# Nyström attention, layer norm and MLP on one core: group 1's transposes moved from DMA to TensorE, k sums of three batches moved from VectorE to GpSimd, and part of the schedule reordered

## The chip, the core and the metric

The kernel runs on one core of a Trainium2 chip. A core has five engines with a queue of instructions each: TensorE (PE in the profile, with its weight loads shown apart as PEld), VectorE (DVE), ScalarE (ACT), GpSimd (POOL) and SyncE (SP), which here issues all DMA transfers. An engine works through its own queue in order and waits where an operand or a buffer is not there yet. The metric is the device time of the core in microseconds (us) for one execution, as a median of repeated runs; 347.5 us before (347.33 to 348.74 in three runs).

## What is computed

Inputs are q, k, v of shape (8, 8, 576, 64) (batches, heads, rows, head size), a scale g of 512, and weights of 512x2048 and 2048x512, all fp32. The reference, cut to what matters:

```python
q_lm = q.reshape(B, H, 32, 18, D).mean(axis=3)       # 32 landmarks, each the mean of 18 rows
k_lm = k.reshape(B, H, 32, 18, D).mean(axis=3)
A  = softmax(q @ k_lm.T / 8)                          # 576 x 32
Bm = softmax(q_lm @ k_lm.T / 8)                       # 32 x 32
C  = softmax(q_lm @ k.T / 8)                          # 32 x 576
Z  = Bm.T / (norm_1(Bm) * norm_inf(Bm))
for _ in range(6):
    Z = 2 * Z - Z @ Bm @ Z
attn = A @ Z @ C @ v                                  # heads are then laid side by side: x is (8, 576, 512)
xn = (x - mean(x)) / sqrt(var(x) + 1e-6) * g_ln       # over the 512 columns
out = x + relu(xn @ w_ch1) @ w_ch2                    # 512 -> 2048 -> 512
```

## The kernel before, in words

The 8 x 576 = 4608 rows of x are cut into 36 blocks of 128 rows (`xblk`), and four blocks make a group: 9 groups for the MLP. A batch of 576 rows is 4.5 blocks. A unit (U = 2 per batch) is half a batch's heads, four heads.

**The MLP stream.** `mlp()` is a generator that runs group after group. For a group it needs the four centred blocks (`xn`) turned so that the 512 columns lie on partitions (`xnT`). Then come 16 x 4 matmuls into `psh` (w_ch1; ACT writes relu of it as `hT`) and 4 x 16 matmuls into `pso` (w_ch2; DVE adds x into `ot`, SP stores it). Each `next` of the generator places about one matmul on PE; `fill(n)` takes n of them. The program thus lays MLP matmuls between the steps of the attention, and the tables `counts` say how many stand after each step. Since every engine keeps program order (`keep_in_program_order`), this writing order is the order of the queues.

**Turning the rows.** Group 0's four blocks are turned by PE (`transpose_block`: four 128x128 transposes into the PSUM tile `psxt`, and a DVE copy into `xnT`). The blocks of all other groups are turned by a DMA transpose (`turn_by_dma`), issued on SP in program order among the loads of q, k and v and the stores of the result. `psh` of a group is not placed before all four turns of it are placed, and reads all four.

**The attention.** Batches 0 and 1 go through `attention`: PE turns q and k (`pst`, with their landmark sums in `pss`), ACT copies them out as `xT`. Batches 2 | 3, 4 | 5, 6 | 7 are four sets that go through `attention2`. For a set, `Coming` prepares the inputs: SP loads a part (one unit of k, q or v) into one of 6 `stg` buffers, POOL casts it to fp16 (`nat`, 8 buffers, or `natv`), DVE turns it (`turn`: `xT`), and the landmark sums are made: those of q by five POOL additions (`asum`, `s16`), of which DVE turns the small result; those of k by one DVE reduction (`add_up`: `lmk`). `next_cast` places one cast (and one load ahead of it), `next_job` one `turn` or `add_up`; the loop over `sets` calls both after each step of the set before. In `attention2` come first the scores (`psb`, `psec`, exponentials on ACT, `bm` and `ecT` on DVE), then `psse` and `pscv`, then six steps of the iteration (`psn` on PE, `st` and `ebd` on DVE, each needing the one before; `psea` and its exponential in the first), `pszc`/`zcbd`, and the rows of the batch (`psy` on PE, `xblk` on DVE).

**Layer norm.** When a block of rows is whole, `block_done` places its mean and variance and its centring. Blocks 4 to 7 (group 1) are done by ACT in `center_by_act`: a mean pass and a subtraction (`xn`), and a pass of squares (`junk`) for the variance. Later blocks with an even number are summed by ACT in two passes (`stats_by_act`), the others by DVE (`bn_stats`), and POOL centres them (`center`). `deviations` (ACT: `lnv`, `rstd`) gives a group's scales, needed by its `ot`. What is placed on the list `later` is written out by `settle()` after the step.

**The start.** Ahead of the sets stands an order written out by hand: the steps of batch 0 (`a0`), batch 1 (`a1`), `scale_w1` (w_ch1 times g, cast to fp16 in slices of 256 columns by ACT and POOL) and `fill`. For group 0 a `psh` tile holds 2 x 256 columns and takes 8 matmuls.

## Time and profile before

| | |
|---|---|
| time, median of 3 runs | 347.5 us (347.33 to 348.74) |
| the profiled execution's own time | 347.76 us |
| its span (first to last instruction) | 345.9 us |
| PE busy | 317.6 us, 92% of the span |
| DVE, ACT, POOL busy | 183.0, 148.9, 136.1 us |
| mean granted TensorE clock | 0.979 of full speed |

The span lies 1.9 us under the execution's own time. The page cuts the span into 40 slices of 8.6 us and gives each engine's busy share in tenths; the windows view gives busy time, count of instructions and granted clock (PEclk) for stretches that one chooses. The timeline lists instructions in order of time as: start, duration, engine, line, operation, output and inputs, count, and in brackets how long the engine sat idle before it and what ended that. Nearly all instructions are recorded through helpers, so they bear the lines 67 (other engines) or 73 (PE), and have to be told apart by their tiles' names. Rows of one kind in a run are merged; the duration of a merged row of matmuls has the tail of the pipeline in it.

### The profile page before, as it was taken

To read this page: it belongs to the slowest core of one execution; us is meant where nothing else is said; L and a number is where in the kernel's file an instruction comes from. 1 tells how busy PE (TensorE), PEld (TensorE's weight loads), DVE (VectorE), ACT (ScalarE), POOL (GpSimd) and SP (SyncE) were. 2 spreads that over 40 slices of the span, in tenths; PEclk is the share of its full clock that TensorE was granted. 3 is DMA by queue.
4 is the path that set the end of the run, shared out by engine and by line. 5 is a ranking of instruction groups with operands and counts; after the bars stand their busy time and mean duration, and the time that the engine had idled before them with its cause. 6 is when DMAs were issued, how large, how long until landed. Compare 5 with 4: busy or idle time off the path is not lost.

```text
span 345.9 us, 8196 instructions
## 1 busy us (share of the span) xinstructions
PE 317.6 (92%) x3396; PEld 158.9 (46%) x3396; DVE 183.0 (53%) x393; ACT 148.9 (43%) x294; POOL 136.1 (39%) x214
## 2 busy tenths in 40 slices
PE   7787989686899999699999999999999999999994
PEld 6545764232344544244454544545444444444441
DVE  2556569562996738998454656872346510020011
ACT  3339855901546057027830474465116405504600
POOL 3488879999999829623101001430002300000000
PEclk9989999986999999999999999999999999999999
DMA  7999999999798886027102401450135034022023
GB/s 269 366 355 364 348 408 288 291 284 310 266 353 120 241 213 181 0 59 139 31 4 63 96 2 27 95 79 17 30 73 81 0 81 88 15 61 63 0 53 68
DMA packets 38932, 50.86 MB, mean 147 GB/s; under 512 B 20464, under 2 KB 24560, under 8 KB 38896
## 3 DMA queue, kind: packets, MB, share of 16 engines
q1 hardware_dynamic: 38896, 50.35, 51.6%
q8 instruction: 26, 0.43, 0.5%
q14 instruction: 10, 0.08, 0.1%
HBM read 36.70 MB, written 9.44 MB: 133 GB/s over the span
## 4 chain that ended last, share of the span: by engine, by line
PE 66%; DVE 14%; ACT 4%; DMA 2%; POOL 2%; issue 2%; SPq 0%; POOLq 0%
PE psh L73 31%; PE pso L73 28%; DVE ebd L67 3%; DVE st L67 2%; DVE xT L67 2%; PE pscv L73 2%; DMA stg<-in_v_dram 2%; PE psy L73 2%; DVE lmk L67 2%; DVE xblk L67 1%; ACT xn L67 1%; POOL asum L67 1%; PE psec L73 1%; PE psea L73 1%; POOL nat L67 1%
## 5 line engine op out<-in xcount | busy, mean ns | idle before, releaser
L73 PE MATMUL psh<-xnT,w 128*128 128x512 f16 (+1 forms) x640 | 136.4, 361 | 5.8 <-issue 4.3
L67 ACT ACTIVATE hT<-psh 128x512 f16<-128x512 f32 x144 | 85.1, 597 | 121.1 <-PE psh L73 120.6
L73 PE MATMUL pso<-w,hT 128*128 128x512 f16 x576 | 133.0, 381 | 0.0
L73 PEld LDWEIGHTS <-w 128*128 128x128 f16 x640 | 59.8, 98 | 62.3 <-issue 9.3
L73 PEld LDWEIGHTS <-hT 128*128 128x128 f16 x576 | 54.9, 98 | 61.3 <-issue 2.6
L67 DVE SCALAR_TENSOR_TENSOR ot<-pso,rstd,xblk 128x512 f32<-128x512 f32 x36 | 26.9, 748 | 80.4 <-PE pso L73 80.3
L67 POOL CAST nat<-stg 128x1152 f16<-128x1152 f32 x28 | 32.3, 1169 | 3.9 <-DMA stg<-in_k_dram 1.9
L67 POOL CAST natv<-stg 128x1152 f16<-128x1152 f32 x16 | 18.4, 1172 | 31.9 <-PE pscv L73 21.7
L67 DVE TENSOR_TENSOR xblk<-psy,rcpd 128x512 f32<-128x512 f32 (+1 forms) x40 | 27.6, 691 | 2.1
L67 DVE SCALAR_TENSOR_TENSOR st<-st,psn 128x192 f16<-128x192 f16 (+3 forms) x36 | 14.3, 397 | 23.0 <-PE psn L73 23.0
L67 POOL TENSOR_SCALAR negm<-mvg 128x1 f32<-128x1 f32 x18 | 3.5, 192 | 55.1 <-DVE mvg L67 46.6
L67 DVE TENSOR_TENSOR ebd<-st,mask 128x256 f16<-128x256 f16 (+1 forms) x30 | 22.7, 756 | 1.0
L67 POOL TENSOR_TENSOR asum<-asum 128x256 f32<-128x256 f32 (+2 forms) x36 | 20.4, 566 | 2.8
L67 POOL TENSOR_SCALAR xn<-xblk,mvg 128x512 f16<-128x512 f32 x10 | 6.9, 694 | 35.8 <-ACT junk L67 35.8
L73 PE MATMUL psy<-zcbd,ea 128*128 128x260 f16 (+1 forms) x80 | 16.5, 283 | 3.0 <-ACT xT L67 1.2
L67 DVE STREAM_TRANSPOSE xT<-nat 128x576 uint32<-128x576 uint32 x24 | 18.4, 766 | 0.0
L67 DVE TENSOR_REDUCE lmk<-xT 128x64 f16<-128x1152 f16 x12 | 16.1, 1342 | 0.1
L67 ACT ACTIVATE junk<-xblk 128x512 f16<-128x512 f32 x10 | 6.3, 628 | 22.4 <-DVE xblk L67 22.4
L67 POOL TENSOR_TENSOR asum<-nat 128x576 f32<-128x576 f16 x12 | 15.4, 1282 | 1.0
L67 DVE BATCH_NORM_STATS2 st<-xblk 128x6 f32<-128x512 f32 x22 | 15.2, 691 | 0.6
L67 POOL TENSOR_SCALAR xn<-xblk,negm 128x512 f16<-128x512 f32 x18 | 12.5, 694 | 3.3 <-DMA xnT<-xn 1.7
L73 PEld LDWEIGHTS <-ea 128*128 128x128 f16 (+1 forms) x80 | 7.2, 101 | 14.0 <-issue 4.9
(107 smaller groups left out, 247.7 us busy)
## 6 DMA issues: line engine op xcount, KB each, us to landing
stg<-in_q_dram SPq DMA_DIRECT2D x16, 576.0 KB, 6.8
stg<-in_k_dram SPq DMA_DIRECT2D x16, 576.0 KB, 7.8
out_dram<-ot SPq DMA_DIRECT2D x72, 128.0 KB, 2.4
stg<-in_v_dram SPq DMA_DIRECT2D x10, 576.0 KB, 7.5
w1stg<-in_moe_w_ch_dram SPq DMA_DIRECT2D x16, 256.0 KB, 6.1
w2stg<-in_moe_w_ch_dram SPq DMA_DIRECT2D x16, 256.0 KB, 4.9
stg<-in_v_dram SPq DMA_DIRECT2D x12, 288.0 KB, 6.5
xnT<-xn SPq DMA_TRANSPOSE x32, 3.4
```

The lines of the kernel that those rows point to most:

```text
L67: return lambda *args, **kw: keep(getattr(self.engine, op)(*args, **kw))
L73: keep(nc.tensor.matmul(o, l, r, start=start, stop=stop, tile_position=(rb, cb), skip_group_check=(skip or cb != 0)))
```

## The change

1. `center_by_act` no longer issues a DMA transpose for group 1. Its blocks are turned by PE in `transpose_block(1, u)`, from two places in `mlp()`: within the last two `pso` rows of group 0 at every eighth matmul, if the block's `xn` is placed, and ahead of group 1's `psh` otherwise. ACT copies these four `psxt` tiles into `xnT`. Each such turn takes one place in `fill`.
2. The squares of blocks 4 to 7, group 1's `deviations`, and the sums and the centring of block 8 are put on a list `late`, of which one entry is placed per step from step 3 of batch 2's `attention2` on.
3. For the sets (5, 6) and (7) the landmark sums of k are made by POOL as those of q are (`k_by_pool`). Their casts are spread over the steps of the set before (`spread`), none is placed earlier than that set, and their `turn` jobs begin at step 5 (before: step 1). `s16` has 8 buffers (before: 6). Before, `next_cast` went on to the set after the next when the next was done.
4. At the start, group 0's first three `psh` tiles and `scale_w1(0)` to `(2)` are placed ahead of most of batch 1's `pst`/`pss` steps, and the two rows of batch 0 that begin group 0 come first.
5. Four numbers of the second row of `counts` go from 17, 17, 17, 15 to 16, 16, 15, 14. `zeros` is half as wide, read more often to the same width.

The diff, without the lines for `zeros` and `s16`:

```diff
 
 
     class Coming:
-        def __init__(self, bs, first_by_pool=0):
-            self.bs, self.first_by_pool = bs, first_by_pool
+        def __init__(self, bs, k_by_pool=False):
+            self.bs, self.k_by_pool = bs, k_by_pool
             self.units = [(b, u) for b in bs for u in range(U)]
             pairs = [(w, w + 1) for w in range(0, len(self.units), 2)]
             self.parts = [(nm, w) for pair in pairs for nm in ("k", "q") for w in pair]
...
             for i, (nm, w) in enumerate(self.parts):
                 if nm != "v":
                     self.jobs.append((self.turn, i))
-                if nm == "k" or nm == "q" and w < first_by_pool:
+                if nm == "k" and not k_by_pool:
                     self.jobs.append((self.add_up, i))
+            self.done, self.turned = 0, set()
             self.stg, self.n16, self.sums, self.xT, self.lm = {}, {}, {}, {}, {}
 
+
+        def spread(self, step):
+            return self.done * 18 >= (step + 1) * len(self.parts)
+
         def next_job(self):
-            if self.jobs:
+            if self.jobs and (self.jobs[0][1] in self.n16 or self.jobs[0][1] in self.turned):
                 f, i = self.jobs.pop(0)
+                self.turned.add(i)
                 f(i)
 
         def load(self, i, queue=nc.sync):
...
                 self.lm = {nm: asm.tile([P, 4, LM, 2], FP16, name="lm" + nm,
                                         tag="lm" + nm) for nm in ("q", "k")}
             stg = self.stg.pop(i)
+            self.done += 1
             if nm == "v":
                 natv_of[b] = natv_buf[b % NV][:].rearrange("p a j e -> p (a j) e")
                 assert b - NV in v_used
...
             t = nat.tile([P, SEG, D], FP16, name="nat", tag="nat")
             pool.tensor_copy(out=t[:], in_=stg[:])
             self.n16[i] = t
-            if nm == "q" and w >= self.first_by_pool:
+            if nm == "q" or self.k_by_pool:
                 s = asum.tile([P, NJ, D], FP32, name="asum", tag="asum")
-                s16 = asm.tile([P, D], FP16, name="s16", tag="s16", bufs=6)
+                s16 = asm.tile([P, D], FP16, name="s16", tag="s16", bufs=8)
                 self.sums[i] = s16
                 for o, x, y in ((s[:], t[:, 0:9, :], t[:, 9:18, :]),
                                 (s[:, 0:4, :], s[:, 0:4, :], s[:, 4:8, :]),
...
             later.append(lambda: center_by_act(j))
         else:
             if by_act(j):
-                later.append(lambda: stats_by_act(j))
+                (late if j == 8 else later).append(lambda: stats_by_act(j))
             else:
                 stats(j)
-            later.append(lambda: center(j) if g <= mlp_at[0] + 1
+            (late if j == 8 else later).append(lambda: center(j) if g <= mlp_at[0] + 1
                          else uncentered.setdefault(g, []).append(j))
-        if u == 3:
+        if u == 3 and g != 1:
             later.append(lambda: deviations(g))
 
 
     mlp_at, uncentered = [0], {}
 
 
-    later = []
+    later, late = [], []
 
     def settle():
         while later:
...
         act(xn[:], x_blk[j][:], AF.Copy, scale=-1.0 / DM, accum_out=negm[:])
         act(xn[:], x_blk[j][:], AF.Identity, bias=negm[:], scale=1.0)
         if by_act(j):
-            junk = mxn.tile([P, DM], FP16, name="junk", tag="junk", bufs=1)
-            act(junk[:], x_blk[j][:], AF.Square, bias=negm[:],
-                accum_out=mvgs[g][:, u, 1:2])
-        if g > 0:
-            turn_by_dma(j)
+            def squares():
+                junk = mxn.tile([P, DM], FP16, name="junk", tag="junk", bufs=1)
+                act(junk[:], x_blk[j][:], AF.Square, bias=negm[:],
+                    accum_out=mvgs[g][:, u, 1:2])
+            late.append(squares)
+            if u == 3:
+                late.append(lambda: deviations(g))
 
     def center(j):
         g, u = divmod(j, 4)
...
     xnTs = {}
 
 
-    def transpose_block(u):
+    def transpose_block(g, u):
         if u == 0:
-            xnTs[0] = mxnT.tile([P, KCH, 512], FP16, name="xnT", tag="xnT")
-        xn = xn_of.pop(u)
+            xnTs[g] = mxnT.tile([P, KCH, 512], FP16, name="xnT", tag="xnT")
+        xn = xn_of.pop(4 * g + u)
         psxt = psM.tile([P, KCH, P], FP16, name="psxt", tag="pm")
         for c in range(KCH):
             TR(psxt[:, c, :], xn[:, ts(c, P)], ident16[:])
-        dve.tensor_copy(out=xnTs[0][:, :, ts(u, P)], in_=psxt[:])
+        if g == 0:
+            dve.tensor_copy(out=xnTs[g][:, :, ts(u, P)], in_=psxt[:])
+        else:
+            scalar.copy(xnTs[g][:, :, ts(u, P)], psxt[:])
+        turned.setdefault(g, []).append(u)
 
     turned = {}
 
...
                 for u in (0, 2):
                     if u == 0:
                         for i in range(2):
-                            transpose_block(i)
+                            transpose_block(0, i)
                             yield True
                     for m0 in range(0, MCH, 2):
                         if u == 0 and m0 in (6, 10):
-                            transpose_block(2 if m0 == 6 else 3)
+                            transpose_block(0, 2 if m0 == 6 else 3)
                             yield True
                         if u == 0 and m0 < MCH - 6:
                             scale_w1(m0 // 2 + 3)
...
                         yield True
             else:
                 while len(turned.get(g, ())) < 4:
-                    yield False
+                    u = len(turned.get(g, ()))
+                    if g == 1 and 4 + u in xn_of:
+                        transpose_block(1, u)
+                        yield True
+                    else:
+                        yield False
                 xnT = xnTs.pop(g)
                 for j in uncentered.pop(g + 1, ()):
                     center(j)
...
                        start=(m == 0), stop=(m == MCH - 1))
                     if m < MCH - 1:
                         yield True
+                    if g == 0 and u >= 2 and m % 8 == 3:
+                        n = len(turned.get(1, ()))
+                        if 4 + n in xn_of:
+                            transpose_block(1, n)
+                            yield True
                 ot = mout.tile([P, DM], FP32, name="ot", tag="ot")
                 dve.scalar_tensor_tensor(out=ot[:], in0=pso[:], scalar=rstds[g][:, u:u + 1],
                                          in1=x_blk.pop(j)[:], op0=ALU.mult, op1=ALU.add)
...
     for _ in range(6):
         run(a0)
         warm(1, 512)
-    run(a0, a1, a0, a0)
-    run(a1)
+    run(a0, a0, a0, a1)
     scale_w1(0)
     fill(1)
-    run(a0)
+    scale_w1(1)
+    fill(1)
+    scale_w1(2)
+    fill(4)
     run(a1)
-    fill(1)
-    scale_w1(1)
-    run(a1)
-    scale_w1(2)
+    fill(4)
+    run(a0, a1)
     fill(4)
     run(a0)
     fill(4)
     for _ in a0:
         pass
     run(a1)
-    fill(10)
+    fill(4)
+    run(a1)
+    fill(4)
     cast_v(1)
     fetch_w2()
     run(a1)
...
     settle()
 
 
-    sets = [Coming((2,)), Coming((3, 4)), Coming((5, 6)), Coming((7,))]
+    sets = [Coming((2,)), Coming((3, 4)), Coming((5, 6), True), Coming((7,), True)]
     to_load = [(c, i) for c in sets for i in range(len(c.parts))]
     to_cast = list(to_load)
 
...
 
 
     counts = [[10, 14, 14] + 6 * [6] + [4] + 3 * [6] + 2 * [9],
-              [12, 12, 17, 17, 17, 15] + 6 * [6] + [5] + 4 * [6] + 6 * [9],
+              [12, 12, 16, 16, 15, 14] + 6 * [6] + [5] + 4 * [6] + 6 * [9],
               [12, 12, 20, 20, 20, 17] + 6 * [9] + [9] + 10 * [8],
               [14, 21, 21] + 6 * [10] + [10] + 5 * [9]]
     for c, after, count in zip(sets, sets[1:] + [None], counts):
         for step, _ in enumerate(attention2(c.bs, c)):
             fill(count[step])
             settle()
-            next_cast()
-            if after and step >= 1:
+            if late and step >= 3:
+                late.pop(0)()
+            if after and after.done < len(after.parts) and not (
+                    after.k_by_pool and after.spread(step)):
+                next_cast()
+            if after and step >= (5 if after.k_by_pool else 1):
                 after.next_job()
         while after and after.jobs:
             fill(8)
```

How the queues move is shown at three places. The first is ACT at the start, from batch 0's first rows to the first `hT` and its follower (`xn` centres a block of group 0, `xT` is a turned q or k of batch 1 copied out, `w_16` a slice of w_ch1, `hT` the relu of a `psh` tile). Before:

```order
L67 COPY xT_746<-pst_736 128x1152
L67 ACTIVATE w1_16_157<-w1stg_162,g_sb_80 128x256
L67 ACTIVATE xn_777,negm_776<-xblk_769 128x512
L67 ACTIVATE xn_777<-xblk_769,negm_776 128x512
L67 COPY xT_790<-pst_780 128x1152
L67 ACTIVATE w1_16_157<-w1stg_166,g_sb_80 128x256
L67 COPY xT_830<-pst_811 128x1152
L67 ACTIVATE w1_16_157<-w1stg_170,g_sb_80 128x256
L67 ACTIVATE w1_16_157<-w1stg_174,g_sb_80 128x256
L67 ACTIVATE hT_761<-psh_840 128x2x256
```

Now:

```order
L67 ACTIVATE xn_699,negm_698<-xblk_690 128x512
L67 ACTIVATE xn_699<-xblk_690,negm_698 128x512
L67 COPY xT_725<-pst_715 128x1152
L67 ACTIVATE w1_16_157<-w1stg_162,g_sb_80 128x256
L67 ACTIVATE w1_16_157<-w1stg_166,g_sb_80 128x256
L67 ACTIVATE w1_16_157<-w1stg_170,g_sb_80 128x256
L67 ACTIVATE w1_16_157<-w1stg_174,g_sb_80 128x256
L67 ACTIVATE hT_740<-psh_766 128x2x256
L67 COPY xT_786<-pst_776 128x1152
```

The slices of w_ch1 and the first `hT` stand ahead of the copies of batch 1; on PE the first three `psh` tiles stand between batch 1's turns in the same way, and 44 instead of 34 of `psh`'s 256-column matmuls stand ahead of batch 1's `psb`, 76 instead of 64 ahead of its `psse`.

The second is ACT between block 7's centring and the first exponentials of batch 2. Before (`lnv` and `rstd` are group 1's deviations, the last two `junk` rows block 8's sums):

```order
L67 ACTIVATE xn,negm<-xblk 128x512
L67 ACTIVATE xn<-xblk,negm 128x512
L67 ACTIVATE junk,mvg<-xblk,negm 128x512
L67 ACTIVATE lnv<-mvg,eps_ln 128x2 x2
L67 ACTIVATE rstd<-lnv 128x4
L67 ACTIVATE junk,mvg<-xblk 128x512
L67 ACTIVATE junk,mvg<-xblk,mvg 128x512
L67 ACTIVATE psb<-psb 128x64
L67 ACTIVATE ec<-psec 128x576 x2
```

Now:

```order
L67 ACTIVATE xn,negm<-xblk 128x512
L67 ACTIVATE xn<-xblk,negm 128x512
L67 COPY xnT<-psxt 128x4x128
L67 ACTIVATE psb<-psb 128x64
L67 ACTIVATE ec<-psec 128x576 x2
L67 COPY xnT<-psxt 128x4x128 x3
L67 ACTIVATE hT<-psh 128x512 x2
L67 ACTIVATE ea<-psea 128x576 x2
L67 ACTIVATE hT<-psh 128x512
L67 ACTIVATE junk,mvg<-xblk,negm 128x512
```

The squares of blocks 4 to 6, each behind its own `xn` before, are gone from this stretch too; they come one at a time after batch 2's first `psea`. On PE the four turns of group 1 stand among the last 28 `pso` of group 0, the last of them four `pso` ahead of group 1's first `psh`; 9 `psh` (before: 7) stand ahead of batch 2's first `psn`. The four DMA_TRANSPOSE of group 1 are gone from SP.

The third is POOL, from the casts of batch 3's and 4's v on (`natv`). Before (`nat` begins the parts of batches 5 and 6; `xn` is block 8):

```order
L67 CAST natv1_115<-stg_1470 128x18x64
L67 TENSOR_SCALAR xn_1864<-xblk_1539,mvg_1546 128x512
L67 CAST natv1_115<-stg_1503 128x18x64
L67 CAST natv0_113<-stg_1535 128x18x64
L67 CAST natv0_113<-stg_1560 128x18x64
L67 CAST nat_1982<-stg_1650 128x1152
L67 CAST nat_2004<-stg_1771 128x1152
L67 CAST nat_2028<-stg_1878 128x1152
L67 TENSOR_TENSOR asum_2030<-nat_2028 128x576
```

Now (the `xn` are blocks 8 to 11):

```order
L67 CAST natv1_115<-stg_1469 128x18x64
L67 CAST natv1_115<-stg_1499 128x18x64
L67 CAST natv0_113<-stg_1528 128x18x64
L67 CAST natv0_113<-stg_1551 128x18x64
L67 TENSOR_SCALAR xn_2065<-xblk_1532,mvg_1539 128x512
L67 TENSOR_SCALAR negm_2089<-mvg_1539 128x1
L67 TENSOR_SCALAR xn_2091<-xblk_2071,negm_2089 128x512
L67 TENSOR_SCALAR xn_2115<-xblk_2095,mvg_1539 128x512
L67 TENSOR_SCALAR negm_2139<-mvg_1539 128x1
L67 TENSOR_SCALAR xn_2141<-xblk_2121,negm_2139 128x512
L67 CAST nat_2273<-stg_1646 128x1152
L67 TENSOR_TENSOR asum_2275<-nat_2273 128x576
```

The parts of batches 5 and 6 stand behind the centring of group 2, and each of their eight k and q parts is followed by its five additions. On DVE, four reductions of k are replaced by four turns of a 128x32 tile, and the last two turns of q stay where they were, behind the sixth `st` of batches 3 and 4.

6 lines of the change are left out of this document (3 added, 3 removed).

## The prediction

> **What bounds the kernel now.** I read the page's slices first: PE's busy tenths, and under them the granted clock.
>
> ```profile
> PE   7787989686899999699999999999999999999994
> PEclk9989999986999999999999999999999999999999
> ```
>
> PE is full from slice 12 (95 us) to the end, but for one 6 near 140 us; the last slice is the drain. Before that it has holes, and the clock falls to 8 and 6 in slices 9 and 10. The windows view says what the full part means:
>
> ```profile
> 180.00:190.00 10.00, 10.00 (x185) 4.97 (x184) 4.88 (x6) 0.00 (x0) 2.24 (x2) 1.00 0.24 54
> ```
>
> The columns are: stretch, its length, then PE, PEld, DVE, ACT, POOL busy (instructions), clock, DMA share, GB/s. PE is busy for all ten microseconds and nobody else is. So the end is set by PE's work plus PE's idle and slow time, and a change gains what it takes from the holes before 100 us and near 140 us, less what it adds to PE. The holes stand in PE's timeline:
>
> ```profile
> 64.21 2.33 PE L73 MATMUL pso<-w,hT 128*128 128x512 f16 x10
> 68.34 0.20 PE L73 MATMUL psse<-bm,bones 128*128 128x64 f16 x1 [1.80 <-DVE bm L67]
> ...
> 70.05 4.20 PE L73 MATMUL pso<-w,hT 128*128 128x512 f16 x14
> 74.18 0.89 PE L73 MATMUL pscv<-natv,ecT 32*32 32x65 f16 x72
> 75.00 1.68 PE L73 MATMUL pso<-w,hT 128*128 128x512 f16 x7
> 80.98 3.14 PE L73 MATMUL psh<-xnT,w 128*128 128x512 f16 x7 [4.30 <-issue]
> ...
> 84.22 1.16 PE L73 MATMUL psea<-xT,lmk 32*32 32x512 f16 x32
> ```
>
> There are two waits, 1.80 and 4.30 us, and behind each the same matmuls take longer. The windows of 1 us show why (clock is the third number from the end):
>
> ```profile
> 69.00:70.00 1.00, 0.88 (x72) 0.72 (x72) 0.90 (x5) 0.00 (x0) 0.84 (x3) 0.50 1.52 196
> 72.00:73.00 1.00, 1.00 (x5) 0.39 (x4) 0.65 (x1) 0.00 (x0) 0.92 (x2) 0.94 0.92 355
> 79.00:80.00 1.00, 0.00 (x0) 0.00 (x0) 0.00 (x0) 0.00 (x0) 0.92 (x2) 0.50 0.97 350
> 85.00:86.00 1.00, 1.00 (x27) 0.46 (x12) 0.82 (x2) 0.56 (x2) 0.84 (x3) 0.61 1.05 390
> ```
>
> The clock is halved from about 69 to 72 us and from 79 to 85.6 us, each time after a wait.
>
> What ends the waits? For the long one, SP's queue and the landing time of `xnT`:
>
> ```profile
> 64.83 1.75 SPq L822 DMA_TRANSPOSE xnT<-xn  x1
> ...
> 73.88 1.23 SPq L822 DMA_TRANSPOSE xnT<-xn  x1
> DMA to landing us min/median/max: 2.4/3.4/7.0
> ```
>
> Group 1's last transpose is issued at 73.88, among loads that wait for buffers, and lands up to 7.0 us later: 80.9, where `psh` starts. The profile calls this wait "issue"; the sum of issue and landing names it. For the short one, ACT's queue:
>
> ```profile
> 64.58 0.71 ACT L67 ACTIVATE junk<-xblk,negm 128x512 f16<-128x512 f32 x1
> ...
> 65.29 0.47 ACT L67 ACTIVATE lnv<-mvg,eps_ln 128x2 f32<-128x2 f32 x2
> ...
> 65.90 0.61 ACT L67 ACTIVATE junk<-xblk 128x512 f16<-128x512 f32 x1
> ...
> 67.36 0.20 ACT L67 ACTIVATE psb<-psb 128x64 f32<-128x64 f32 x1
> ```
>
> Batch 2's `psb` is on PSUM before the `pso` of 64.21, but its exponential waits behind squares, deviations and block 8's sums; `bm` and `psse` follow it.
>
> **The change part by part.** Three rows give full-clock prices: a 512-column matmul is 13.81/64 = 0.216 us (a row of the chain of waits), 32 score matmuls 0.70, a turn of one block 0.39 with its tail.
>
> ```profile
> 272.18 13.81 PE pso L73 x64
> 134.24 0.70 PE L73 MATMUL psea<-xT,lmk 32*32 32x512 f16 x32
> 27.99 0.39 PE L77 MATMUL psxt<-ident,xn 128*128 128x128 f16 x4
> ```
>
> *The short wait.* From 64.58 to 67.36 ACT now does 2.8 us that moves behind; one copy of a turned block comes in (0.6, as an `hT` of the same size). So `psb` comes 2.2 us earlier or more, over 1.80: the wait goes. With the wait goes the halved clock: 4.20 - 14 x 0.216 = 1.2 and 1.14 (the `pscv` at 68.97) is 0.25 over the 0.89 of its twin at 74.18. Gain 1.8 + 1.45. The moved passes land behind batch 2's `psea`, where ACT has waited for PE; the deviations are wanted only by group 1's `ot`, near 100 us.
>
> [...]
>
> *The long wait.* The transposes leave SP; PE turns the blocks. The last turn stands four `pso` (0.86 us) ahead of `psh`, and ACT's copy (0.6) fits in. Gain 4.3, and the halved clock behind it: 3.14 - 7 x 0.216 = 1.6, and 1.16 - 0.70 = 0.46. Together 6.4. What could be late next is the `xn` of block 7, which even now is done when its squares start at 64.58.
>
> *PE's new work.* Sixteen transposes: 4 x 0.24 (their weight loads alone) to 4 x 0.39. I take 1.2, nearer the lower end, since the tail overlaps what follows.
>
> *The start.* Here the trace shows the pieces but not their new order.
>
> ```profile
> 31.18 1.11 ACT L67 COPY xT<-pst 128x1152 f16<-128x1152 f16 x1
> 32.18 0.91 ACT L67 ACTIVATE w<-w1stg,g_sb 128x256 f16<-128x256 f32 x2
> ...
> 37.88 0.22 ACT L67 ACTIVATE psb<-psb 128x64 f32<-128x64 f32 x1
> 41.29 0.22 PE L73 MATMUL psse<-bmT 32*32 32x32 f16 x8
> 44.52 1.20 PE psh L73 x10
> ```
>
> (The first three rows are ACT's timeline, then PE's, then the chain of waits.) ACT is the bound here: before its `psb` it idles little. In the new order ACT begins with a block's `xn` at about 24.1 and has until `psb` three pairs of `xn` (1.45 each), four `xT` (1.0), eight `w` (0.45), five `hT` (0.5): 14.5 us, and I count 0.8 us of waiting for the first `psh` and for the third row of batch 0. So `psb` comes at 39.4, 1.5 later than now. Then 32 `psh` (now 30 and a turn, in 5.1 us) bring `psse` to 44.4, 3.1 later. Of these, 12 `psh` more are done, 12 x 0.12 = 1.45, which need not be done later. Lost: 1.65. The iteration of batch 1 then runs 3 us deeper into POOL's casts (one `ebd` of it takes 1.33 us beside them, others 0.43): 0.5. PE is sparser at 21 to 24, so the slower clock that slice 3 shows (8) may last longer: 0.3. I take a loss of 2.4. Bounds: a gain of 1.0, if the new order closes holes that PE has there now (the 8 and 7 of slices 3 and 4); a loss of 4.0, if the `xT` copies hold up the shared PSUM buffers once more.
>
> *k sums on POOL.* Two lines group what DVE loses and gets:
>
> ```profile
> L67 DVE TENSOR_REDUCE lmk<-xT 128x64 f16<-128x1152 f16 x12 | 16.1, 1342 | 0.1
> L67 DVE STREAM_TRANSPOSE lmq<-s 128x32 uint32<-128x32 uint32 x12 | 2.0, 168 | 0.0
> 142.02 0.34 PE L73 MATMUL psn<-st,ebd 128*128 128x96 f16 x4 [1.92 <-DVE ebd L67]
> ```
>
> Six of twelve reductions go, six small turns come. Only those inside the iteration of batches 3 and 4 matter, where PE waits for DVE (1.92 us the longest). Two of the four reductions of that set stand in it now; the other two lie ahead, where DVE is idle, but their turns now move into it. By count DVE's chain there shortens by 0.8 us. I take 0.4 (bounds: a loss of 3.3, below, and a gain of 3, all the waiting there). Batch 7's sums fall behind 150 us, where PE is full as at 180: nothing.
>
> *POOL's order.* The centring of group 2 now stands ahead of batches 5 and 6:
>
> ```profile
> 104.81 0.18 DVE L67 BATCH_NORM_AGGREGATE mvg<-st 128x2 f32<-128x6 f32 x1
> 99.22 1.15 POOL L67 CAST nat<-stg 128x1152 f16<-128x1152 f32 x1
> 103.80 1.14 POOL L67 CAST nat<-stg 128x1152 f16<-128x1152 f32 x1
> 138.92 1.14 POOL L67 CAST nat<-stg 128x1152 f16<-128x1152 f32 x1
> 144.07 0.32 POOL L67 TENSOR_TENSOR s<-asum 128x64 f16<-128x64 f32 x1
> 148.66 0.77 DVE L67 STREAM_TRANSPOSE xT<-nat 128x576 uint32<-128x576 uint32 x1
> ```
>
> How far ahead is the rest by then? 9.65 of gains less 1.2, 2.4 and 0.43 (two `psh` more stand ahead) is 5.6 at batch 2's rows; five matmuls fewer stand ahead of the iteration of batches 3 and 4 (1.08), and with the 0.4 it is 7.1 at its end. So POOL waits for block 11's mean (104.8 now, 99.2 then), centres, and casts and sums from 100.6 on. A part costs 4.58 (99.22 to 103.80) to 5.47 (138.92 to 144.39): eight end at 137 to 144. DVE wants the last at 148.66 - 7.1 = 141.6. With half of them slow it is 140.8: no wait. Nothing, then, but with a margin under 1 us.
>
> *The rest.* The five matmuls taken from `counts` are done later on a full PE, the narrower `zeros` streams the same columns: nothing.
>
> Sum: 1.8 + 1.45 + 6.4 - 1.2 - 2.4 + 0.4 = 6.4. The profiled execution took 347.76, of which 345.9 is the span and 1.9 lies around it, which stays. **347.76 - 6.4 = 341.3 us**; the median of the runs is 0.3 under the profiled one, so a median may come out at 341.0.
>
> **The rivals.** *The start costs nothing* (or gains): then 9.65 - 1.2 + 0.4 = 8.9 remain, 338.9. For it: the first `psh` could start near 27.5, ahead of two `xT` copies that it waits behind now. Against: ACT's total up to `psb` does not shrink.
>
> *DVE is slowed by POOL.* `ebd` varies though its work does not:
>
> ```profile
> L67 DVE TENSOR_TENSOR ebd<-st,mask x30: 424/692/1802, 42.6 to 255.6; 128x256 f16<-128x256 f16 x18, 128x512 f16<-128x512 f16 x12
> ```
>
> In batches 3 and 4 it takes 0.69 or 1.61 to 1.80, the long ones while POOL makes its first addition of a part. Two of five are long now; were all, the iteration would lengthen by 3 x 1.1 = 3.3: 341.3 + 0.4 + 3.3 = 345.0. Against: POOL is as busy there now. [...]
>
> *POOL becomes the pace* (the slower side). Each microsecond that the last sum comes after 141.6 holds DVE ahead of batch 3's first row, and PE with it once its few `pso` are through. The gain is gone when the sum ends at 148, that is at (148 - 100.6)/8 = 5.9 us a part; at 6.2 it ends at 150.2 and the time is 341.3 + 8.6 = 349.9, PE's clock not yet counted. For it: POOL's additions stretch beside DVE, 4.58 to 5.47. Against: 5.9 has not been seen.
>
> *It does not do what it says:* the wait for group 1 only moves, because batch 2's iteration, brought forward, waits for POOL's casts of batches 3 and 4, whose pace DMA sets. Then what the start loses and PE adds decides: about 347.5. Against: DVE wants them 10 us and more after they are made.
>
> **How the numbers follow.** Forecast 0.52; the start for nothing 0.18; DVE slowed 0.12; POOL the pace 0.08; only moved 0.06; the rest spread. The likeliest one's own range is 339.5 to 343.5. To 8 in 10 it takes in the first rival and its gain of 1.0 at the low end (337.5) and the second at the high end (345.5). Half a per cent, about what a measurement can tell from no change here, is 1.7 us: faster is below 345.8, which the forecast, the first and nearly all of the second rival give: 0.83; within it 0.09; slower 0.08.
>
> **What would show it.** Right: no wait over 0.5 us ahead of `psse` and of group 1's first `psh`, the clock at 1.00 from 60 to 90 us, batch 2's first `psea` near 79.1 instead of 84.22. The start: batch 1's `psse` at 44.4 instead of 41.29; if at 42.8 or earlier, it cost nothing. POOL: the eighth sum of batches 5 and 6 before 141.6, and no DVE wait for it. Wrong: halved clock anywhere behind 28 us, or PE waiting over 4 us between 125 and 155.

## The result, and the profile after

The changed kernel takes 338.25 us (median of four executions, 336.97 to 338.75) against 347.52 for the kernel before: a ratio of 0.972, 95% interval 0.9685 to 0.9756, or 9.3 us less. Forecast were 341.3, and 6.4 less. The execution profiled took 338.48 us with a span of 336.7. The ratios here leave out executions more than 1.5% above the fastest of their kernel, which matters only for the kernel with both waits back, below: its twelve times lie in two bunches (344.03 to 346.80 and 348.83 to 349.48), and four of the upper bunch are left out of its ratio.

The slices of its page, PE and granted clock:

```profile
PE   7778899799999997989999999999999999999994
PEclk9976999999999999999999999999999999999999
```

The clock falls once, in slices 3 and 4 (17 to 34 us), and not again. The deep holes near 70 and 80 us are gone; shallow ones (a 7 or an 8) are left near 63, 130 and 147 us. PE's timeline at the places that the prediction spoke of:

```profile
56.91 0.58 PE L73 MATMUL psy<-zcbd,ea 128*64 128x260 f16 x2
...
66.44 0.69 PE L73 MATMUL psec<-xT,lmq 32*32 32x512 f16 x28 [1.09 <-DVE xblk L67]
69.23 0.19 PE L73 MATMUL psse<-bm,bones 128*128 128x64 f16 x1
...
75.12 2.11 PE L73 MATMUL psh<-xnT,w 128*128 128x512 f16 x9
77.24 0.70 PE L73 MATMUL psea<-xT,lmk 32*32 32x512 f16 x32
...
149.71 1.46 PE L73 MATMUL psh<-xnT,w 128*128 128x512 f16 x6 [1.09 <-DMA xnT<-xn]
```

Neither `psse` of batch 2 nor group 1's first `psh` waits, and the `psea` behind them is at full rate (0.70). Two waits of 1.09 us stand out now: `psec` behind a row block of batch 1 (0.44 before), and group 3's first `psh` behind a DMA transpose (0.20 before).

The windows view, one microsecond each (the clock is the third number from the end, the DMA share the next):

```profile
22.00:23.00 1.00, 0.80 (x4) 0.36 (x3) 0.53 (x3) 0.00 (x0) 1.00 (x4) 0.50 1.10 348
...
30.00:31.00 1.00, 1.00 (x16) 1.00 (x15) 0.00 (x0) 0.64 (x2) 0.90 (x3) 0.50 1.11 369
...
32.00:33.00 1.00, 1.00 (x19) 0.95 (x18) 0.34 (x2) 0.80 (x2) 0.94 (x3) 1.00 1.05 392
```

Here the clock is halved until 31.7 us, where the kernel before had it back at 24.3. The chain of waits, by engine:

```profile
PE 64%; POOL 16%; DVE 10%; DMA 6%; issue 2%; ACT 0%; SPq 0%; POOLq 0%; DVEq 0%
```

POOL's sums of batches 5 and 6 have become part of the chain that ended last. That says where the chain runs, not what the sums cost; the experiments below take them out.

### The profile page after: what moved, and what is told of

The parts are those of the page before. It is cut to its first block, busy times and chain, and to the rows that moved or that the text cites. A ratio compares the mean times of both kernels' runs of the same rounds, so it can differ in the third digit from the quotient of the medians.

```text
span 336.7 us, 8234 instructions
## 1 busy us (share of the span) xinstructions
PE 316.0 (94%) x3412; PEld 160.4 (48%) x3412; DVE 173.2 (51%) x393; ACT 150.4 (45%) x298; POOL 154.8 (46%) x244
## 4 chain that ended last, share of the span: by engine, by line
PE 64%; POOL 16%; DVE 10%; DMA 6%; issue 2%; ACT 0%; SPq 0%; POOLq 0%; DVEq 0%
PE psh L73 30%; PE pso L73 27%; POOL asum L67 8%; DMA stg<-in_q_dram 5%; POOL nat L67 4%; PE pscv L73 2%; DVE xT L67 2%; DVE lmk L67 2%; PE psy L73 1%; DVE st L67 1%; DVE xblk L67 1%; DVE ebd L67 1%; POOL natv L67 1%; DMA xnT<-xn 1%; POOL s L67 1%
## 5 line engine op out<-in xcount | busy, mean ns | idle before, releaser
L67 POOL TENSOR_TENSOR asum<-asum 128x256 f32<-128x256 f32 (+2 forms) x54 | 28.3, 524 | 4.2
L67 POOL TENSOR_TENSOR asum<-nat 128x576 f32<-128x576 f16 x18 | 23.9, 1326 | 1.5
L67 DVE TENSOR_TENSOR ebd<-st,mask 128x256 f16<-128x256 f16 (+1 forms) x30 | 20.4, 680 | 1.0
L67 ACT ACTIVATE junk<-xblk 128x512 f16<-128x512 f32 x10 | 6.3, 628 | 21.5 <-DVE xblk L67 21.5
L67 DVE RECIPROCAL rcpd<-psy 128x8 f32<-128x8 f32 (+1 forms) x40 | 7.8, 196 | 15.1 <-PE psy L73 15.0
L67 POOL TENSOR_SCALAR xn<-xblk,negm 128x512 f16<-128x512 f32 x18 | 12.5, 696 | 3.5 <-DMA xnT<-xn 1.9
```

The source lines that it names most:

```text
L67: return lambda *args, **kw: keep(getattr(self.engine, op)(*args, **kw))
```

## The experiments

Twelve kernels ran, in three sets of four; each set shared its runs of the kernel before. The table gives them as ratio to that kernel; a thousandth is 0.35 us. Medians are over all executions. Where two kernels are compared by ratio, "either way" joins the two 95% intervals.

| kernel | median us | ratio, 95% interval |
|---|---|---|
| changed kernel (at first) | 338.25 | 0.972 [0.9685, 0.9756] |
| changed kernel again | 338.23 | 0.9729 [0.9701, 0.9758] |
| group 1 turned by DMA | 347.49 | 1.0002 [0.9983, 1.0022] |
| squares at their old place | 343.19 | 0.9865 [0.9831, 0.9900] |
| both of these | 347.82 | 0.9966 [0.9927, 1.0005] |
| old start | 339.81 | 0.9781 [0.9760, 0.9803] |
| old start, six places of the stream more | 336.34 | 0.9686 [0.9655, 0.9717] |
| changed kernel, start with more idle matmuls | 337.02 | 0.9702 [0.9672, 0.9733] |
| k sums and cast order as before | 337.68 | 0.9711 [0.9687, 0.9735] |
| old start + six, k sums on DVE in POOL's new order | 339.14 | 0.9756 [0.9714, 0.9799] |
| old start + six, k sums and cast order as before | 335.91 | 0.9654 [0.9611, 0.9697] |
| the last, with more idle matmuls | 337.61 | 0.9713 [0.9668, 0.9758] |
| new start with idle matmuls, k sums and order as before | 338.24 | 0.9727 [0.9685, 0.9768] |

### The two waits

Group 1 by DMA again:

```diff
@@ center_by_act
         act(xn[:], x_blk[j][:], AF.Identity, bias=negm[:], scale=1.0)
+        if g == 1:
+            turn_by_dma(j)
```

> The changed kernel with group 1's blocks turned by DMA again; the postponed squares, the start and the k sums stay. Theory (the long wait was SP's: the last of group 1's transposes is issued at about 74 us behind loads that wait for buffers, whatever ACT does ahead of it): group 1's first psh starts at 80 to 82 us instead of 75.12 in the changed kernel, after a wait of 4 us or more, and the clock is halved for some 3 us behind it; 5 to 6 us of wait plus 2.1 of halved clock less 1.2 for the sixteen transposes that PE is spared: 344 to 346 us against 338.25. Rival (the squares held up the transposes: ACT's xn of blocks 5 to 7 come earlier without them, and so do the transposes): psh without a wait over 1 us, 337 to 339 us. Rival (the gain stems from elsewhere and the wait is made up later at the iteration): 339 to 342 us.

The squares at once:

```diff
-            late.append(squares)
+            squares()
-                late.append(lambda: deviations(g))
+                deviations(g)
@@ block_done: block 8's two passes go to later, not to late
```

> The changed kernel with the squares and deviations of group 1 and the passes of block 8 at their old places; the rest stays. Theory (ACT's queue ahead of batch 2's psb is a price of its own): four squares of 0.71, the deviations (1.1) and block 8's two passes (1.2) stand ahead of psb again, which comes at 70 to 72 us instead of 66.77, psse of batch 2 waits 1.5 us or more and the clock is halved behind it: 1.8 + 1.45 by the prediction's sum, 341.5 us, and up to 344 if the copies of the turned blocks, which stand behind the squares too, hold up group 1's psh. Rival (the wait ahead of psse was only a shadow of the later one, and what is lost there is not missed): within 0.8 us of the changed kernel, 337.5 to 339.

The two edits together:

> The changed kernel with both undone at once: group 1's blocks turned by DMA, and squares, deviations and block 8 at their old places. Undone one at a time they cost 9.2 us (DMA turns, 347.49) and 4.9 us (squares, 343.19). Theory (the two waits stand one behind the other, and time saved ahead of the long one is waited away there, since what ends it is SP's queue): 347.5 to 348.5 us, no slower than the DMA turns alone by more than 1. The prediction's sum, which books the two apart (3.25 for the short wait, 6.4 less 1.2 for the long one): 338.25 + 8.45 = 346.7. Rival (two separate losses that add up): 338.25 + 9.2 + 4.9 = 352.4.

With the DMA turns alone put back, the whole gain is gone (1.0002), more than any of the three expectations had. PE's timeline, and SP's:

```profile
69.89 0.19 PE L73 MATMUL psse<-bm,bones 128*128 128x64 f16 x1
...
82.38 5.58 PE L73 MATMUL psh<-xnT,w 128*128 128x512 f16 x13 [7.41 <-DMA xnT<-xn]
```

```profile
73.92 1.18 SPq L105 DMA_DIRECT2D stg<-in_v_dram  x2
75.19 1.19 SPq L808 DMA_DIRECT2D out_dram<-ot  x2
76.47 2.06 SPq L837 DMA_TRANSPOSE xnT<-xn  x1
```

`psse` comes without a wait, since the squares are still out of the way, and the time saved is waited away at `psh`: 7.41 us instead of 4.30. The last transpose is issued behind loads and stores on SP's queue, though ACT's `xn` for it was done at 67.1. From within this wait the clock is halved (0.50 in each of five windows of 1 us between 80 and 87 us), and the thirteen `psh` take 5.58 us, where they take 2.97 at full clock (below). With the squares back alone (PE turning), the time lies in the range of the theory. PE's timeline shows the other wait, and `psh` 5.3 us later than in the changed kernel, of which 0.8 stem from ahead of batch 1's first row (57.67 against 56.91; this execution was the slowest of its six):

```profile
72.26 0.20 PE L73 MATMUL psse<-bm,bones 128*128 128x64 f16 x1 [2.10 <-DVE bm L67]
...
80.38 2.10 PE L73 MATMUL psh<-xnT,w 128*128 128x512 f16 x9
```

ACT's timeline names the cause: the exponential stands behind block 8's second pass, and comes at 71.28 where the changed kernel has it at 66.77.

```profile
70.56 0.72 ACT L67 ACTIVATE junk<-xblk,mvg 128x512 f16<-128x512 f32 x1
71.19 0.19 ACT L67 ACTIVATION_READ_ACCUMULATOR junk<-xblk,mvg 128x1 f32 x1
71.28 0.20 ACT L67 ACTIVATE psb<-psb 128x64 f32<-128x64 f32 x1
```

With both back, both waits are there. The long one is shorter here, and the clock stays up behind it; but this is the fastest of the twelve executions (344.03, the median is 347.82):

```profile
69.51 0.20 PE L73 MATMUL psse<-bm,bones 128*128 128x64 f16 x1 [1.62 <-DVE bm L67]
...
79.53 2.97 PE L73 MATMUL psh<-xnT,w 128*128 128x512 f16 x13 [2.74 <-DMA out_dram<-ot]
```

From the ratios: with both waits back the kernel is 0.9966 - 0.9729 = 0.0237 behind the changed one, 8.2 us (1.7 either way); by the medians it is 9.6. Of the 8.2 the turns bring 3.5 by themselves (0.9966 to 0.9865), the postponed squares by themselves nothing (0.9966 to 1.0002), and the squares bring 4.7 once the turns are made. So the waits stand in series: what is saved ahead of the long one pays only when the long one is gone too. The theory's number for both back (347.5 to 348.5) fits the median, 347.82, but by its ratio this kernel is at 346.5, near the number of the prediction's sum (346.7). The rival of two separate losses (352.4) is out.

### The start

The changed kernel once more, as the measure for the next three:

> The changed kernel once more, beside the next three on the same chip and with more executions: 338.25 us as before (337.5 to 339). Its four executions so far went from 336.97 to 338.75; if the spread comes from where the halved clock of the start falls, the times go with the mean clock of each execution.

It gave the same median, 338.23. The times lean with the clock but do not follow it, as four of the six show: 337.19 at 0.988, 338.35 at 0.987, 337.70 at 0.982, 339.98 at 0.973.

The old start, the steps as in the kernel before (36 places of the stream until batch 1's last steps, where the new start has 42):

```diff
-    run(a0, a0, a0, a1)
+    run(a0, a1, a0, a0)
+    run(a1)
     scale_w1(0)
     fill(1)
...
-    fill(4)
-    run(a1)
-    fill(4)
+    fill(10)
     cast_v(1)
```

> The changed kernel with the old order of the start (the steps of batches 0 and 1, the slices of the first weights and the matmuls between them as before); the rest stays. The prediction's sum has the new start cost 2.4 us: 335.9 us. The trace of the changed kernel (batch 1's rows 2.32 us later, 1.30 us of matmuls more done by then) has it cost 1.0: 337.2. Rival (the new start costs nothing, or gains, since its first matmuls of the MLP come early): 338.3 or more. The clock: halved only up to about 24 us as before, where the new order has it halved to 31.

339.81: the old start is 1.6 us slower, 1.8 by ratio (1.2 either way). Both losses that were expected of the new start miss, and the rival's "338.3 or more" holds: the new start as a whole gains. Nor was the old start's clock back at 24 us, but at 28. Its profiled execution was the fastest of seven (338.01). Behind the start it shows a new loss, ACT's `hT` late at the end of group 1's first half:

```profile
93.49 1.46 PE L73 MATMUL pso<-w,hT 128*128 128x512 f16 x6 [1.10 <-ACT hT L67]
```

So the old order again, with as many places as the new one:

```diff
-    fill(10)
+    fill(16)
     cast_v(1)
```

> The changed kernel with the old order of the start, but with six matmuls more (fill of 16 in place of 10) ahead of batch 1's last steps, so that as many of the MLP's matmuls stand ahead of everything behind as in the changed kernel. The old start as it was took 339.81 us, 1.6 more than the changed kernel, though the trace has it ahead. If it is the order itself (waits of ACT and DVE) that loses: 339.8 again. If the six matmuls are what counts (with them short, group 1's turns and psh come too early for ACT, a wait of 1.1 us at its first pso): 337 to 338.2. The prediction's sum (the new order loses 2.4): 335.9.

336.34: now the old order is 1.9 us faster than the new one (0.9686 against 0.9729: 1.5 us, with as much either way). Two things were in one edit of the start: six places of the stream more, worth 3.3 us (0.9781 to 0.9686, 1.3 either way), and the new order, which costs about 1.5. Four of the six are taken by group 1's turns, which `fill` counts like matmuls. Six matmuls are 1.3 us of PE. Of the other 2 us the traces show hints: without the six, the 1.10 of the row above, and batch 2's iteration (first `psea` to first row) 0.7 longer, 12.52 against 11.86 us. That these make up the 2 us is not shown.

Is the order's cost ACT's, or the clock's? Some sixteen idle matmuls keep the clock up in the new order (1.00 in every window from 19 to 36 us):

```diff
-    for _ in range(6):
+    for i in range(6):
         run(a0)
-        warm(1, 512)
-    run(a0, a0, a0, a1)
+        warm(2 if i > 1 else 1, 512)
+    run(a0)
+    warm(2, 512)
+    run(a0)
+    warm(3, 512)
+    run(a0)
+    warm(3, 512)
+    run(a1)
     scale_w1(0)
     fill(1)
+    warm(2, 512)
     scale_w1(1)
     fill(1)
+    warm(2, 512)
```

> The changed kernel with some twenty more idle matmuls of 512 columns in TensorE's holes between 17 and 28 us (their results are not used), to keep the clock up; the rest stays. Theory (the halved clock from 21 to 31 us costs what its longer matmuls show: two rows of eight psh at 1.86 and 1.38 instead of 1.04, two pst and pss rows at half rate): clock 1.00 from 20 us on, 336.3 to 337.3 us, and a smaller spread. Rival (ACT and DVE set the pace there, and the matmuls' rate is hidden; executions of the kernel with the old start took 340.0 at a clock of 1.00 as at 0.99): within 0.5 of the changed kernel. Second rival (the extra matmuls hold up those that are waited for): 0.5 to 1.5 slower.

The first row of batch 1, in PE's timeline of the changed kernel (second profile), of this kernel, and of the old order with six places more:

```profile
56.75 0.58 PE L73 MATMUL psy<-zcbd,ea 128*64 128x260 f16 x2
```

```profile
55.02 0.58 PE L73 MATMUL psy<-zcbd,ea 128*64 128x260 f16 x2
```

```profile
54.89 0.58 PE L73 MATMUL psy<-zcbd,ea 128*64 128x260 f16 x2
```

and the window from 26 to 27 us of the same three:

```profile
26.00:27.00 1.00, 0.26 (x3) 0.26 (x4) 0.96 (x3) 1.00 (x4) 0.90 (x2) 0.50 1.10 348
```

```profile
26.00:27.00 1.00, 0.62 (x6) 0.13 (x3) 0.93 (x3) 1.00 (x2) 0.90 (x3) 1.00 1.10 347
```

```profile
26.00:27.00 1.00, 0.62 (x6) 0.43 (x7) 0.93 (x3) 1.00 (x2) 0.89 (x3) 1.00 1.10 346
```

The same three at batch 1's `psse`, with 76 `psh` done by then in each:

```profile
43.78 0.22 PE L73 MATMUL psse<-bmT 32*32 32x32 f16 x8
```

```profile
42.75 0.22 PE L73 MATMUL psse<-bmT 32*32 32x32 f16 x8
```

```profile
42.71 0.22 PE L73 MATMUL psse<-bmT 32*32 32x32 f16 x8
```

In these traces, with the clock up, the new order reaches `psse` within 0.04 us of the old one and batch 1's rows within 0.13, and both spans are 334.7; with the clock halved the rows come 1.73 later. So close a fit is in part chance, since traces of one order differ by about 1 us at the rows: four with the old order and six places more have them at 54.89 to 55.82, two with the new order and the clock up at 54.05 and 55.02, six with the new order and the clock halved for 6.8 or 10.2 us at 55.40 to 57.67. Place by place that puts the loss on the clock, and none on the order of ACT's work. The times say it less sharply: 337.02 against 338.23 (0.9 us by ratio, 1.4 either way), and the spread is no smaller. The same comparison without POOL's k sums (this edit and the one that puts all k sums back, shown below) does not confirm it:

> The changed kernel with its new start and the idle matmuls that keep the clock at 1.00 there, and with the k sums of batches 5 to 7 on VectorE. Theory (the new order of the start costs only through the clock, and with the clock kept up the two orders end alike: batch 1's rows at 55.02 and 54.89 us, spans of 334.7 both): the same time as the kernel with the old start and six matmuls more, within 0.5 us. Rival (the order of ACT's work costs 1.65 by the prediction, and the clock only 0.3): 1.3 to 2 us slower than that kernel.

338.24, as slow as without the idle matmuls (0.9727 against 0.9711), and 2.3 us behind the old order (335.91). Its trace is 2.4 us ahead at the last rows of batch 2 (93.29 against 95.66 with the k sums back and no idle matmuls) and loses it behind: 0.94 us in a gap of PE at 123.85 that is treated below, and 1.35 waiting for group 3's transposes. That the halved clock delays the new order at the start is what these traces show (the four of the old order, halved for 3.4 us or not at all, show no such delay); that keeping it up gains time at the end is not shown.

And idle matmuls in the old start (with six places more and the k sums back):

```diff
-        warm(1, 512)
-    run(a0, a1, a0, a0)
+        warm(2 if i > 1 else 1, 512)
+    run(a0)
+    warm(2, 512)
+    run(a1, a0)
+    warm(2, 512)
+    run(a0)
+    warm(2, 512)
     run(a1)
```

> The kernel before it, with some ten more idle matmuls of 512 columns between 17 and 25 us (results not used). With the old start the halved clock of the start was short in most executions (mean clock 0.994 to 1.000 in five of six); if the clock of the start is what made the new start slow, there is little left to gain here: 0 to 0.5 under the kernel without them, and a smaller spread. If the spread (335.9 to 338.9) has another cause, it stays as it is.

337.61 against 335.91: 1.7 us slower (2.0 by ratio, 2.2 either way; five of its six times lie above all six without the idle matmuls). The spread is 3.3 us (336.05 to 339.39), against 1.9 without them. Nothing was gained, then, and the spread has another cause than the clock of the start. Its trace, of the slowest of the six executions, shows a gap of 2.17 us, taken up in the section on the hardware.

### k sums and POOL's order

Everything of this part undone, on the new start:

```diff
-    sets = [Coming((2,)), Coming((3, 4)), Coming((5, 6), True), Coming((7,), True)]
+    sets = [Coming((2,)), Coming((3, 4)), Coming((5, 6)), Coming((7,))]
```

> The changed kernel with the k sums of batches 5 to 7 on VectorE and the casts in the old order (batches 5 and 6 ahead of the centring of group 2, as early as the buffers let them); the rest stays. The prediction's sum: 0.4 us slower, 338.65. Reading of the trace, where the iteration of batches 3 and 4 runs 1.2 us shorter than before with the sums on GpSimd: 339.5. Rival (GpSimd, busy from 97 to 137 us with these sums, is the pace, and hands group 3's blocks over late: a wait of 1.09 us at 149.71): its relief gains about that wait, 337.2.

337.68, 0.9711: no loss, and the gain of 0.6 us is inside the intervals. The same edit on the old start with six places more, which leaves of the change only the turns, the postponed squares and the small items of its point 5:

> Of the change only the turns by TensorE and the postponed squares are left: the old start, with six matmuls more (16 in place of 10) ahead of batch 1's last steps, and all k sums of batches 5 to 7 on VectorE with the casts in the old order. The same with the k sums on GpSimd took 336.34 us. If the k sums on GpSimd gain the prediction's 0.4: 336.7. If they cost nothing and gain nothing: 336.3 within 0.5. If GpSimd's sums hold up group 3's blocks (a wait of 0.8 to 1.15 us ahead of group 3's first psh in every trace with them, none with VectorE's): that wait goes, 335.3.

335.91, 0.9654 against 0.9686: again no loss, 1.1 us less with 1.9 either way. This is the fastest kernel here, 12 us under the kernel before. The trace of the first of the two shows what POOL's relief does. SP's queue in the changed kernel, then in this one:

```profile
141.81 1.23 SPq L835 DMA_TRANSPOSE xnT<-xn  x1
143.09 0.57 SPq L105 DMA_DIRECT2D stg<-in_q_dram  x1
143.76 1.19 SPq L835 DMA_TRANSPOSE xnT<-xn  x1
145.04 1.23 SPq L808 DMA_DIRECT2D out_dram<-ot  x2
146.37 1.24 SPq L835 DMA_TRANSPOSE xnT<-xn  x1
```

```profile
141.20 2.68 SPq L835 DMA_TRANSPOSE xnT<-xn  x2
143.98 1.22 SPq L808 DMA_DIRECT2D out_dram<-ot  x2
145.29 1.25 SPq L835 DMA_TRANSPOSE xnT<-xn  x1
```

In the changed kernel POOL's sums end at 137.2, the casts of v fall between the centrings of group 3, and a load between the transposes: the third is issued 1.1 us later (0.6 of it is the lead that the second trace has at batch 3's first row), and `psh` waits the 1.09 shown above. With the sums on DVE and no idle matmuls added it does not wait, on the new start or the old. POOL's sums do not settle that wait, though: the two kernels with idle matmuls and the sums on DVE have it too (1.35 and 1.02), and the old start without the six places, with the sums on POOL, has none. On the other side stands DVE. In the iteration of batches 3 and 4 two reductions of 1.34 us are back, but beside POOL's sums `ebd`, the same instruction five times, is slower: 1.54, 0.83, 0.69, 1.24 and 1.49 us in the changed kernel, 1.51, 0.85, 0.69, 0.69 and 0.69 with the sums on DVE. That takes back 1.4 of the 2.7 us. From its first `psea` to batch 3's first row the iteration lasts 14.53 us with the sums on POOL and 14.29 with them on DVE. Both trades together come to nothing that can be measured.

Last, the k sums alone on DVE, in POOL's new order:

```diff
-                if nm == "k" and not k_by_pool:
+                if nm == "k":
...
-            if nm == "q" or self.k_by_pool:
+            if nm == "q":
```

> The old start with six matmuls more, with GpSimd's new order of casts and centring kept but the k sums of batches 5 to 7 on VectorE: it parts the k sums from the order. If the wait ahead of group 3's first psh comes from GpSimd's sums (4.6 to 5.4 us a part, 1.14 without sums), it goes here as with the old order: 335.3 to 336. If it comes from the new order (the casts spread out, so that v's casts stand between the centrings of group 3): it stays at about 1 us, 336.3. If the six reductions of 1.34 us now press into the iteration of batches 3 and 4: 337 to 339.

339.14, 0.9756: 2.4 us slower than with the sums on POOL (1.9 either way). The third expectation held in size (339 at most), at another place. In the new order the turns and reductions of batches 5 and 6 begin five steps into the set, and the reductions reach batch 3's rows, where PE waits for `xblk`:

```profile
140.66 0.39 PE L73 MATMUL psy<-zcbd,ea 128*128 128x260 f16 x2 [0.88 <-DVE xblk L67]
142.76 0.39 PE L73 MATMUL psy<-zcbd,ea 128*128 128x260 f16 x2 [0.41 <-DVE xblk L67]
145.98 0.40 PE L73 MATMUL psy<-zcbd,ea 128*128 128x260 f16 x2 [0.89 <-DVE xblk L67]
```

So moving the sums to POOL pays for what the later order costs DVE, and nothing beyond that is measured.

## Why the prediction was right, and where its steps were wrong

The time lay in the wide range (337.5 to 345.5) and on the side forecast, 3 us under the likeliest value and below that value's own range (339.5 to 343.5). Step by step:

- **The two waits, 9.65 less 1.2 for PE's turns.** The mechanism was right, and so was the sum: 8.45 forecast, 8.2 measured by ratio when both are put back (9.6 by the medians). Wrong was to book them apart, as 3.25 and 5.2. The squares alone are worth nothing and the turns alone 3.5, since the two waits stand one behind the other. Two terms were a little large: 4.20 and 3.14 hold the tail of their rows and 14 x 0.216 and 7 x 0.216 do not (rows of 14 and 7 at full clock take 3.20 and 1.69), 0.35 us in all; and the four turns take 0.91 on PE, not 1.2. The changed trace shows both waits gone and `psea` of batch 2 at 77.24, not 79.1.
- **The halved clock behind the short wait, 1.45.** It went with the wait. In the changed kernel the clock is at 1.00 from 33 us on, and in the kernel with DMA turns, which lacks only the short wait, the rows behind `psse` are at full rate (14 `pso` at 70.77 in 3.20 us, 72 `pscv` at 73.90 in 0.75). That the clock would go with the wait was an estimate from the order of the two in the trace of before, and it came out so. No run removed the wait and kept the halved clock.
- **The start, a loss of 2.4.** This step failed, and by more than the whole miss: undone exactly, the new start is worth a gain of 1.6 to 1.8. The slip is in one reading. The forecast has ACT's `psb` at 39.4, and with the clock up it comes there, at 39.49. But the 5.1 us then added up to `psse` are counted from PE's `psb` of before (36.18 to 41.29), while ACT's stood at 37.88, 3.4 us ahead of `psse`. With 3.4 the forecast is 42.8 instead of 44.4, 1.5 later than before, and the twelve `psh` done more by then pay for just that: no loss, by the prediction's own sign ("42.8 or earlier"). So the trace with the clock up has it, 42.75. That the changed kernel's 44.28 met the forecast 44.4 is luck: there the halved clock makes up the difference, 1.0 to 1.5 us in the two profiles, for which I had set 0.3. The 0.5 for the iteration beside POOL's casts did not come either; it ran 0.67 shorter than before. And the twelve `psh`, which are the six places of the stream, were credited with their time on PE, 1.45, where they are worth 3.3. In the prediction's terms: 1.45 less 3.9 forecast, 3.3 less 1.5 measured. What is left of the order's 1.5 with the clock up the times do not settle (0.5 with 1.5 either way in one pair of kernels, 2.5 with 2.1 in the other).
- **k sums, a gain of 0.4; POOL's order, nothing.** Together measured as a loss of 0.6 and of 1.1 us, neither told from zero. The eighth sum ended at 137.2, before 141.6, as forecast, with DVE's turn of it at 137.9, 0.7 us behind: the margin under 1 us was real. Not foreseen is the wait for group 3's transposes, 1.09 us. The count for DVE left out what `ebd` loses beside POOL's sums, 1.4 us.
- **Batch 2's iteration.** From its first `psea` to the first full row, 13.44 us before and 11.66 after; 0.46 was credited. In PE's timeline of before the clock is still halved for some of the six `psh` behind that `psea` (a row of 1.69 us instead of 1.47), 0.2 that I left out, and two waits for `ebd` of 0.81 and 0.82 have become 0.18 and 0.43. All later variants lie between 11.3 and 12.5, so most of it belongs to none of the parts put back here.
- **The whole.** Put back each by itself on the changed kernel, both waits (8.2), the start (1.8) and the k sums with POOL's order (-0.6) add up to 9.4 us, which is what the changed kernel gains by its ratio (0.9729); with such intervals the fit is closer than it need be. Against the forecast of 6.4 the start is 4.2 better, the k sums 1.0 and the waits 0.2 worse.
- **Signs.** "Halved clock anywhere behind 28 us" came about, at the start, and was a true sign of a wrong step there. PE did not wait over 4 us between 125 and 155 (about 3.4 in the rows of `psn`, `psy` and `psh`).
- **The rivals.** "The start costs nothing" (338.9) is the nearest in time, and in part the right mechanism: the first `psh` started at 27.81, as it said, and at batch 1's rows the order of ACT's work cost nothing once the clock was up. "DVE is slowed by POOL" came about in part: three of five `ebd` were long, not all, and the longest wait for one was 1.10. POOL as the pace did not come about, nor did "only moved": batch 2's iteration did not wait for POOL's casts. The wait that does move, in the kernel with DMA turns, is SP's.

## What to carry to other kernels

Two waits on one path are one entry until each has been removed alone: the first may be worth nothing while the second stands, and its removal makes the second longer. When times of two rows are added, check that both count from the same event: a matmul's row on PE and the exponential of its result on ACT were 1.7 us apart here, which is the 1.65 that the forecast charged to the order of ACT's work. Where a generator deals out work by places, count what takes the places; moved work that needs some displaces other work. And a part of a change that looks free (sums moved to a half-idle engine) is tried without: here the two parts that remove waits, with six places more, are faster than the whole.

## What the runs showed of the hardware

**The clock comes back in steps.** From the one-microsecond windows, the halved stretch at the start lasts 3.4 us in the kernel before (20.9 to 24.3) and with the old start and six places (20.1 to 23.5), 6.8 with the old start (21.5 to 28.3) and in the second profile of the changed kernel (23.7 to 30.6), 10.2 in its first (21.4 to 31.7) and with the DMA turns (22.9 to 33.1): one, two and three times 3.4. The stretches behind the waits of the kernel before fit too, with 3.4 and 6.8 (68.7 to 72.1 and 79.0 to 85.8). Added up from the clock of the windows, a step is 3.40 to 3.42 us in all of these. PE's busy time in the profile does not tell where the clock falls: in the 3.4 us ahead of the fall at 21.4 us of the changed kernel PE was busy for 2.35 us, 69%; and with both waits back the rows behind the wait of 1.62 us are slow (72 `pscv` in 1.11 us and 14 `pso` in 4.60, against 0.75 and 3.20 with the DMA turns), while those behind the longer wait of 2.74 us are not (13 `psh` in 2.97). What makes it fall stays open. The same kernel got two steps in one execution and three in another, so a comparison of single executions at such a place is worth little.

**In five kernels PE stops at a fixed place of its queue.** They show a gap behind 105 us in the middle of a run of alike matmuls, put down to "issue". PE's timeline with idle matmuls in the old start (its slowest execution), and its windows:

```profile
123.81 0.68 PE L73 MATMUL psea<-xT,lmk 32*32 32x512 f16 x25
126.66 0.22 PE L73 MATMUL psea<-xT,lmk 32*32 32x64 f16 x7 [2.17 <-issue]
```

```profile
124.00:125.00 1.00, 0.49 (x25) 0.21 (x10) 0.96 (x2) 0.59 (x2) 0.24 (x2) 1.00 0.94 217
125.00:126.00 1.00, 0.00 (x0) 0.00 (x0) 0.89 (x2) 0.00 (x0) 1.00 (x1) 1.00 1.08 258
```

and in the timelines with idle matmuls in the new start, and with the two parts alone:

```profile
124.77 0.24 PE L73 MATMUL psea<-xT,lmk 32*32 32x64 f16 x13 [1.01 <-issue]
```

```profile
125.06 0.81 PE L73 MATMUL psh<-xnT,w 128*128 128x512 f16 x3 [0.56 <-issue]
```

Counted in the order of the program, ten idle matmuls with their weight loads move the work by 20 instructions and sixteen by 32, and the gap moves from the fourth `psh` behind the last `psea` to the 26th `psea` and to the 20th: in all three it stands at instruction 3516 of PE's queue, as far as the trace holds them. Another, of 0.22 to 1.10 us, stands near instruction 704 at about 20 us in most of the kernels, and one of 0.25 and 0.39 near 3006 in the two kernels with idle matmuls in the new start. The page of the profile shows a DMA queue with the name of instructions, here with idle matmuls:

```profile
q8 instruction: 27, 0.44, 0.5%
```

27 packets of 16 KB, in all 0.44 MB. The DMA engines were full ahead of the gap at 3516 (shares of 1.00 to 1.10 from 122 to 124 us in the five kernels), but that alone does not set its size: with the k sums back on the new start, PE passes 3516 at a share of 1.06 with 0.3 us at most (six `psh` there in 1.77 us instead of 1.47). That PE waits there for its next instructions, and these behind loads, is my guess from the fixed place and this queue; no run moved the loads away, and it is not shown. In the kernel with the old start and idle matmuls its 2.17 us are more than the 1.7 us by which that kernel is slower.

**Left open**: where the 2 us go, beyond six matmuls, that the old start loses without the six places; what makes the clock fall where it does; and what makes single executions of one kernel differ by 2 to 4 us when the clock does not.
